# A second issue order for the first twelve head pairs of a fused attention and MLP kernel

## The chip, the cores and the metric

The kernel runs on one core of a Trainium2 chip. Its time is the device time of one execution in microseconds (us); the medians are over several executions. Five engines work beside each other, each through its own queue in order: TensorE (PE, matmuls), VectorE (DVE), ScalarE (ACT), GpSimd (POOL) and SyncE (SP, which here only issues DMAs). An instruction that waits holds up everything behind it in its own queue.

## What is computed

```python
q_n, k_n = rmsnorm(q, g_q), rmsnorm(k, g_k)          # over head_dim
attn = softmax(q_n @ k_n.T / sqrt(64)) @ v           # 8 batches x 12 heads x 448 tokens x 64
x = attn.transpose(0, 2, 1, 3).reshape(8 * 448, 768)
h = x @ w_in                                         # 768 -> 2048
out = (h * sigmoid(1.702 * h)) @ w_out               # 2048 -> 768, float32
```

## The kernel before

The unit of the attention is a pair of heads of one batch; pair i belongs to batch i // 6, so that the first twelve pairs are batches 0 and 1. A pair passes through these tasks, which the code names by letters (they are declared from line 730 on with `od.add`):

- **L** loads q, k and v of the pair (three DMAs of 224 KB, lines 515 and 518, issued by SP; k of pair 0 by ACT). **S** squares q and k (line 525 on ACT or 522 on POOL), **R** sums the squares (534, DVE), **Q** makes the inverse root: for pairs 0 to 5 by logarithm and exponential on ACT (545, 546), later for three pairs at once by a seed on DVE (**Q0**, 553 and 555) and eight small instructions on POOL (566 to 569).
- **N** multiplies by it (576, on DVE or POOL, once for q and once for k), **V** casts v (586 on DVE, 589 on POOL), **T** turns q and k (599, PE, for the first twelve pairs; later a DMA transpose, 611), **KQ** and **K** take them to SBUF (603, 606).
- **C** are the scores (643, PE), **E** the exponentials (653 and 651, ACT), **P** the product with v (664, PE), **O** the division (674, 675, DVE), **B** and **X** turn the result into columns of x (690, PE, and 694, DVE; later a DMA transpose, 697). The pairs of batch 0 are worked in two halves of the queries, (C,i,0,..) and (C,i,1,..), the other pairs whole.
- The MLP has **F** (first matmul, 875, 16 blocks of the 2048 columns per batch), **H** (tanh, 885, ACT), **G** (gate, 897, DVE), and for the second matmul **Y** (905) with the first three token tiles, and products P1 to P7 (965) over sums S1 to S5 (956, DVE) and differences TT of the weights (945, DVE) for the others. **WI** and **WO** load w_in and w_out in four parts each (842, 848; POOL issues them, and they land as bf16).

No engine's order is written out by hand. `_Order.run` (line 64) is a small list scheduler that runs while the program is built. Each task has an engine, a planned duration, a key and the tasks that it depends on; when an engine is free in the plan, the ready task with the lowest key is emitted next. What the chip gets is only the resulting order on each queue, with the waits that the data need. Nothing of the planned times is in the program. Three tables steer it: `KEYS` (line 223) gives a task's key, `AT` (line 325) the earliest planned time of a load, and the tasks in `ON` (line 335) go to the other of two engines (S to POOL instead of ACT; N and V to the other of DVE and POOL). Loads and stores are planned with queues of transfers, `share` (line 97) saying how fast each proceeds while others do.

`fill` (line 494) puts dummy matmuls on PE (128x256, line 500) where the plan has a gap ahead of a PE task: 24 and 10 at the very start, and after it

```python
n = idle * FILL / 213 if now < 14000.0 else idle * FILL_GAPS / 110
```

of them. They are real instructions in the queue. Three PSUM banks (`w`) serve T, B, F, Y and the products, one (`o`) serves P, so that a P must wait until DVE has divided the one before it; two pairs of banks (`sc`) serve the scores.

Of the kernel before, what the change touches and what calls it, by code (L numbers as in the profile page):

```python
# [26 lines left out]
class _Order:  # L27
# [36 lines left out]
    def run(self):  # L64
# [26 lines left out]
        queues = {"sw": [], "hw": [], "act": []}  # L91
        moved_to = 0.0
# [4 lines left out]
        def share():  # L97
            n = len(heads())
            return 1.3 / 2 if n == 2 and not queues["sw"] else 1.0 / n

        def next_moved():
            h = heads()
            when = [q[0].there for q in queues.values() if q and q[0].there > moved_to]
            when += [moved_to + t.rest / share() for t in h]
            return min(when) if when else None

        def move_to(now):
            nonlocal moved_to, seq
            while moved_to < now:
                n = next_moved()  # L110
                until = now if n is None else min(now, n)
                h = heads()
                for t in h:
                    t.rest -= (until - moved_to) * share()
# [109 lines left out]
    'g': 14.22, 'gT': -28.28, 'gG': 10.29, ('S', 0, 0): 33.65, ('R', 0, 0): -27.2, ('S', 0, 1):  # L224
    11.09, ('R', 0, 1): 12.24, ('Q', 0): 30.36, ('N', 0, 0): -6.12, ('N', 0, 1): -30.37, ('V',
    0): -7.89, ('T', 0, 0): -31.78, ('T', 0, 1): -29.53, ('KQ', 0): -10.97, ('K', 0): -11.43,
    ('S', 1, 0): 9.57, ('R', 1, 0): -27.21, ('S', 1, 1): 33.28, ('R', 1, 1): 9.51, ('Q', 1):
    33.27, ('N', 1, 0): 9.56, ('N', 1, 1): 11.7, ('V', 1): -5.89, ('T', 1, 0): 57.36, ('T', 1,
    1): 54.48, ('KQ', 1): -6.09, ('K', 1): -5.86, ('S', 2, 0): 32.41, ('R', 2, 0): -5.94, ('Q',
    2): 15.94, ('N', 2, 0): -4.94, ('N', 2, 1): -13.33, ('V', 2): 10.47, ('T', 2, 0): 55.3,  # L230
    ('T', 2, 1): 17.1, ('KQ', 2): -6.5, ('K', 2): -4.7, ('S', 3, 0): -3.51, ('R', 3, 0): -11.44,
    ('Q', 3): 33.8, ('N', 3, 0): -27.91, ('N', 3, 1): -14.89, ('V', 3): -5.47, ('T', 3, 0):
    19.15, ('T', 3, 1): 18.23, ('KQ', 3): 58.1, ('K', 3): -9.14, ('S', 4, 0): 33.8, ('R', 4, 0):
    57.84, ('Q', 4): 34.16, ('N', 4, 0): 23.2, ('N', 4, 1): 9.27, ('V', 4): -10.25, ('T', 4, 0):
    -3.92, ('T', 4, 1): 18.9, ('KQ', 4): -7.69, ('K', 4): 59.82, ('S', 5, 0): 18.65, ('R', 5,
    0): -7.68, ('Q', 5): 22.81, ('N', 5, 0): 1.27, ('N', 5, 1): 43.71, ('V', 5): -16.35, ('T',
    5, 0): -40, ('T', 5, 1): 16.66, ('KQ', 5): -8.39, ('K', 5): -9.71, ('L', 6, 0): 54.32, ('L',
    6, 1): 54.14, ('L', 6, 2): 54.15, ('S', 6, 0): -24.61, ('R', 6, 0): -9.13, ('N', 6, 0):
    -16.87, ('N', 6, 1): -1.42, ('V', 6): -24.19, ('T', 6, 0): -37.32, ('T', 6, 1): 56.1, ('KQ',
    6): -17.12, ('K', 6): -15.91, ('L', 7, 0): 55.06, ('L', 7, 1): 57.25, ('L', 7, 2): 55.05,  # L240
    ('S', 7, 0): -17.15, ('R', 7, 0): 31.45, ('N', 7, 0): 3.06, ('N', 7, 1): -23.94, ('V', 7):
    -24.2, ('T', 7, 0): 52.6, ('T', 7, 1): 22.24, ('KQ', 7): -20.86, ('K', 7): 9.99, ('L', 8,
    0): 54.79, ('L', 8, 1): 57.74, ('L', 8, 2): 53.4, ('S', 8, 0): 44.16, ('R', 8, 0): 31.27,
    ('Q0', 8): -1.5, ('Q', 8): -10, ('N', 8, 0): 3.5, ('N', 8, 1): 19.46, ('V', 8): -20.98,
    ('T', 8, 0): 27.35, ('T', 8, 1): 59.99, ('KQ', 8): -20.38, ('K', 8): -21.01, ('L', 9, 0):
    53.95, ('L', 9, 1): 55.46, ('L', 9, 2): 55.45, ('S', 9, 0): -9.31, ('R', 9, 0): -17.4, ('N',
    9, 0): -3.91, ('N', 9, 1): -10.14, ('V', 9): 22.05, ('T', 9, 0): -32.5, ('T', 9, 1): -35.1,
    ('KQ', 9): 21.57, ('K', 9): -38.08, ('L', 10, 0): 57.72, ('L', 10, 1): 59.75, ('L', 10, 2):
    60, ('S', 10, 0): -10.41, ('R', 10, 0): 19.25, ('N', 10, 0): 27.28, ('N', 10, 1): -1.35,
    ('V', 10): -15.43, ('T', 10, 0): -30.6, ('T', 10, 1): -36.19, ('KQ', 10): -4.09, ('K', 10):  # L250
    -37.28, ('L', 11, 0): 59.99, ('L', 11, 1): 59.99, ('L', 11, 2): 55.44, ('S', 11, 0): -13.26,
    ('R', 11, 0): 29.44, ('Q0', 11): 25.43, ('Q', 11): -9.79, ('N', 11, 0): 24.78, ('N', 11, 1):
    3.73, ('V', 11): 3.33, ('T', 11, 0): -37.35, ('T', 11, 1): -37.08, ('KQ', 11): -32.1, ('K',
    11): 24.13, ('C', 0, 0, 0): -31.61, ('E', 0, 0, 0): 59.86, ('C', 0, 0, 1): -26.54, ('E', 0,
    0, 1): 56.76, ('P', 0, 0, 0, 0): 53.97, ('P', 0, 0, 0, 1): -27.58, ('P', 0, 0, 0, 2):
    -30.53, ('P', 0, 0, 0, 3): -27.58, ('O', 0, 0, 0): -5.47, ('B', 0, 0): -40, ('X', 0, 0):
    -11.15, ('C', 1, 0, 0): -26.72, ('E', 1, 0, 0): -2.87, ('C', 1, 0, 1): 57.55, ('E', 1, 0,
    1): 16.48, ('P', 1, 0, 0, 0): 18.9, ('P', 1, 0, 0, 1): 18.63, ('P', 1, 0, 0, 2): 18.63,
    ('P', 1, 0, 0, 3): 18.89, ('O', 1, 0, 0): -13.5, ('B', 1, 0): 20.2, ('X', 1, 0): -11.33,
    ('C', 2, 0, 0): -40, ('E', 2, 0, 0): 18.66, ('C', 2, 0, 1): 20.21, ('E', 2, 0, 1): 13.02,  # L260
    ('P', 2, 0, 0, 0): 15.34, ('P', 2, 0, 0, 1): -36.54, ('P', 2, 0, 0, 2): -39.14, ('P', 2, 0,
    0, 3): -39.14, ('O', 2, 0, 0): -0.47, ('B', 2, 0): -39.81, ('X', 2, 0): -5.02, ('C', 3, 0,
    0): 17.29, ('E', 3, 0, 0): 39.33, ('C', 3, 0, 1): -39.63, ('E', 3, 0, 1): 38.35, ('P', 3, 0,
    0, 0): 15.85, ('P', 3, 0, 0, 1): 43.01, ('P', 3, 0, 0, 2): 17.41, ('P', 3, 0, 0, 3): 18.15,
    ('O', 3, 0, 0): -10.7, ('B', 3, 0): 15.63, ('X', 3, 0): 0.44, ('C', 4, 0, 0): -4.69, ('E',
    4, 0, 0): 38.96, ('C', 4, 0, 1): 38.48, ('E', 4, 0, 1): 24.48, ('P', 4, 0, 0, 0): -33.37,
    ('P', 4, 0, 0, 1): 60, ('P', 4, 0, 0, 2): -31.73, ('P', 4, 0, 0, 3): 17.26, ('O', 4, 0, 0):
    0.31, ('B', 4, 0): 57.93, ('X', 4, 0): 41.32, ('C', 5, 0, 0): -31.71, ('E', 5, 0, 0): 17.88,
    ('C', 5, 0, 1): 15.57, ('E', 5, 0, 1): 35.94, ('P', 5, 0, 0, 0): 33.77, ('P', 5, 0, 0, 1):
    33.77, ('P', 5, 0, 0, 2): 33.77, ('P', 5, 0, 0, 3): 33.76, ('O', 5, 0, 0): -0.04, ('B', 5,  # L270
    0): -23.85, ('X', 5, 0): 33.63, ('C', 0, 1, 0): 14.17, ('E', 0, 1, 0): 39.32, ('C', 0, 1,
    1): -39.73, ('E', 0, 1, 1): 33.79, ('P', 0, 1, 0, 0): -36.96, ('P', 0, 1, 0, 1): -33.38,
    ('P', 0, 1, 0, 2): 60, ('P', 0, 1, 0, 3): -14.87, ('O', 0, 1, 0): 60, ('B', 0, 1): 54.78,
    ('X', 0, 1): 34.24, ('C', 1, 1, 0): -36.97, ('E', 1, 1, 0): -39.74, ('C', 1, 1, 1): -36.95,
    ('E', 1, 1, 1): 24.11, ('P', 1, 1, 0, 0): 33.76, ('P', 1, 1, 0, 1): -23.7, ('P', 1, 1, 0,
    2): -22.7, ('P', 1, 1, 0, 3): -23.86, ('O', 1, 1, 0): -21.46, ('B', 1, 1): -39.64, ('X', 1,
    1): 0.33, ('C', 2, 1, 0): -27.46, ('E', 2, 1, 0): -31.49, ('C', 2, 1, 1): -18.62, ('E', 2,
    1, 1): 37.85, ('P', 2, 1, 0, 0): -39.65, ('P', 2, 1, 0, 1): -40, ('P', 2, 1, 0, 2): 21.69,
    ('P', 2, 1, 0, 3): -40, ('O', 2, 1, 0): -14.64, ('B', 2, 1): -36.82, ('X', 2, 1): -4.18,
    ('C', 3, 1, 0): 55.19, ('E', 3, 1, 0): 37.86, ('C', 3, 1, 1): 60, ('E', 3, 1, 1): 23.18,  # L280
    ('P', 3, 1, 0, 0): -18.63, ('P', 3, 1, 0, 1): -13.68, ('P', 3, 1, 0, 2): -13.69, ('P', 3, 1,
    0, 3): -11.57, ('O', 3, 1, 0): 39.32, ('B', 3, 1): 22.25, ('X', 3, 1): -18.47, ('C', 4, 1,
    0): -15.41, ('E', 4, 1, 0): 9.01, ('C', 4, 1, 1): -25.6, ('E', 4, 1, 1): -9.3, ('P', 4, 1,
    0, 0): -36.38, ('P', 4, 1, 0, 1): -36.83, ('P', 4, 1, 0, 2): -36.39, ('P', 4, 1, 0, 3):
    -34.65, ('O', 4, 1, 0): -20.37, ('B', 4, 1): 20.64, ('X', 4, 1): 22.61, ('C', 5, 1, 0):
    -16.67, ('E', 5, 1, 0): 42.7, ('C', 5, 1, 1): 51.97, ('E', 5, 1, 1): 36.5, ('P', 5, 1, 0,
    0): 47.97, ('P', 5, 1, 0, 1): 48.4, ('P', 5, 1, 0, 2): 60, ('P', 5, 1, 0, 3): 55.7, ('O', 5,
    1, 0): 25.18, ('B', 5, 1): -40, ('X', 5, 1): 21.57, ('C', 6, None, 0): 24.44, ('E', 6, None,
    0): -11.29, ('E', 6, None, 1): -16.82, ('C', 6, None, 2): 24.41, ('E', 6, None, 2): -7.71,
    ('E', 6, None, 3): -16.82, ('P', 6, None, 0, 0): -40, ('P', 6, None, 0, 1): -40, ('P', 6,  # L290
    None, 0, 2): -40, ('P', 6, None, 0, 3): -39.93, ('O', 6, None, 0): 23.74, ('P', 6, None, 1,
# [933 lines left out]
```

## Time and profile before

| what | us |
|---|---|
| median of four runs (lowest to highest) | 428.72 (428.24 to 429.49) |
| the profiled execution | 428.15 |
| its span from first to last instruction | 426.4 |
| PE busy in the span | 408.8 |
| ACT, DVE, POOL busy | 302.7, 297.1, 189.8 |
| dummy matmuls: 89, of which 55 stand behind the first 34 | |
| first F of batch 1 (marks the end of the stage that the change orders) | 92.83 |

The profile is one execution. A busy share is an average over stages; a "wait" in it is the idle time of an engine ahead of an instruction, with the instruction that ended it. The median of the runs lies 0.57 us over the profiled execution, and the span 1.75 us under it.

### The profile page before, as it was taken

How to read it: one execution, taken by the hardware profiler on the slowest of the kernel's cores; microseconds unless marked ns; L12 is line 12 of the kernel's file. 1: busy time of each engine (PE TensorE's matmuls, PEld its weight loads, DVE VectorE, ACT ScalarE, POOL GpSimd, SP SyncE). 2: the span in 40 equal slices, each digit the busy share in tenths (PEclk: the TensorE clock that was granted, in tenths of full speed). 3: DMA queues.
4: the chain of work that ended last, by engine and by line, in shares of the span. 5: the costliest groups of instructions: out<-in, count | busy, mean ns of one | idle time of the engine just before them, and what ended most of it. 6: DMA issues, size and time to landing. Idle time of an engine off the chain costs nothing.

```text
span 426.4 us, 10048 instructions
## 1 busy us (share of the span) xinstructions
PE 408.8 (96%) x3874; PEld 241.6 (57%) x3874; DVE 297.1 (70%) x584; ACT 302.7 (71%) x437; POOL 189.8 (45%) x277
## 2 busy tenths in 40 slices
PE   6899899999989999999999999999999999999995
PEld 4558686655555555555555555555555555565553
DVE  5967988579988667965787577764676555655663
ACT  4898788869978699978986589967775477604400
POOL 5396843657387473853636345553642100000000
PEclk9999999999999999999999999999999999999999
DMA  8999999375659989666646687566433630121023
GB/s 238 270 259 245 264 251 246 94 163 128 136 118 216 196 208 213 154 166 156 171 102 160 167 220 164 136 139 165 75 77 95 158 90 13 23 67 38 0 75 92
DMA packets 101555, 63.38 MB, mean 149 GB/s; under 512 B 54916, under 2 KB 101508, under 8 KB 101508
## 3 DMA queue, kind: packets, MB, share of 16 engines
q1 hardware_dynamic: 93712, 55.88, 54.0%
q0 software_dynamic: 7296, 6.29, 9.1%
q8 instruction: 30, 0.49, 0.5%
q10 hardware_dynamic: 500, 0.57, 0.4%
q14 instruction: 17, 0.14, 0.1%
HBM read 45.61 MB, written 11.01 MB: 133 GB/s over the span
## 4 chain that ended last, share of the span: by engine, by line
PE 78%; DVE 10%; ACT 5%; issue 3%; DMA 3%; SPq 0%; POOL 0%; DVEq 0%; ACTq 0%
PE w L875 30%; PE w L965 17%; PE o L664 10%; PE sc L643 9%; PE sc L965 4%; PE w L905 4%; DVE late L956 3%; PE sc L875 2%; ACT att L653 2%; DMA raw<-in_k_dram 2%; ACT sq L525 2%; DVE obs L675 1%; DVE ssq L534 1%; DVE g L897 1%; DVE w_out_s L945 1%
## 5 line engine op out<-in xcount | busy, mean ns | idle before, releaser
L651 ACT ACTIVATE att<-sc 112x896 bf16<-112x896 f32 x168 | 145.8, 916 | 33.9 <-PE sc L643 33.4
L875 PE MATMUL w<-xt,w_in_s 128*128 128x448 bf16 (+1 forms) x810 | 150.7, 330 | 0.1
L875 PEld LDWEIGHTS <-w_in_s 128*128 128x128 bf16 x864 | 78.1, 97 | 54.2 <-issue 6.7
L664 PEld LDWEIGHTS <-att 112*128 112x128 bf16 x1536 | 72.5, 98 | 49.3 <-issue 18.2
L576 POOL TENSOR_TENSOR row<-raw,rs 112x512 bf16<-112x512 f32 x80 | 89.5, 1139 | 23.1 <-DMA qk<-row 13.7
L897 DVE SCALAR_TENSOR_TENSOR g<-th,w 128x448 bf16<-128x448 f32 x119 | 72.5, 616 | 27.1 <-ACT th L885 26.5
L885 ACT ACTIVATE th<-w 128x448 f32<-128x448 f32 x119 | 64.7, 548 | 26.6 <-PE w L875 25.1
L589 POOL TENSOR_TENSOR vx<-vraw,ones 112x512 bf16<-112x512 f32 x35 | 36.5, 1042 | 97.9 <-PE o L664 62.0
L664 PE MATMUL o<-vx,att 112*128 112x65 bf16 x1280 | 74.0, 194 | 4.9 <-DVE obs L675 4.8
L534 DVE TENSOR_REDUCE ssq<-sq 112x16 f32<-112x1024 f32 (+1 forms) x50 | 58.4, 1170 | 10.0 <-ACT sq L525 8.8
L525 ACT ACTIVATE sq<-raw 112x1024 f32<-112x1024 f32 (+1 forms) x43 | 44.5, 1035 | 9.7 <-DMA raw<-in_k_dram 5.8
L643 PE MATMUL sc<-qk 64*128 64x448 bf16 (+1 forms) x360 | 46.9, 342 | 1.6 <-DVE qk L606 1.4
L675 DVE TENSOR_TENSOR obs<-o,rcp 112x256 bf16<-112x256 f32 x96 | 40.7, 424 | 3.3
L965 PEld LDWEIGHTS <-g 128*128 128x128 bf16 x336 | 29.9, 97 | 19.6 <-issue 3.0
L674 DVE RECIPROCAL rcp<-o 112x4 f32<-112x4 f32 x96 | 17.0, 177 | 33.2 <-PE o L664 32.6
L965 PEld LDWEIGHTS <-late 128*128 128x128 bf16 x328 | 28.8, 97 | 18.3 <-issue 2.6
L965 PE MATMUL w<-w_out_s,g 128*128 128x384 bf16 x176 | 33.5, 325 | 0.0
L965 PE MATMUL w<-w_out_s,late 128*128 128x384 bf16 x152 | 29.7, 326 | 0.2 <-DVE late L956 0.2
L965 PE MATMUL w<-late 128*128 128x384 bf16 x144 | 28.1, 326 | 0.0
L978 DVE TENSOR_SCALAR osb<-w 128x384 f32<-128x384 f32 x25 | 13.9, 556 | 16.9 <-PE w L965 16.8
L566 POOL TENSOR_TENSOR t<-rs 112x48 f32<-112x48 f32 x28 | 8.2, 292 | 37.3 <-DVE rs L555 36.2
L617 ACT ACTIVATE qk<-qk,gG 128x448 bf16<-128x448 bf16 x36 | 24.2, 676 | 0.7 <-DMA qk<-row 0.7
(92 smaller groups left out, 379.3 us busy)
## 6 DMA issues: line engine op xcount, KB each, us to landing
raw<-in_q_dram SPq DMA_DIRECT2D x44, 224.0 KB, 3.8
raw<-in_k_dram SPq DMA_DIRECT2D x43, 224.0 KB, 4.5
vraw<-in_v_dram SPq DMA_DIRECT2D x42, 224.0 KB, 3.7
w_in_s<-in_moe_w_in_dram POOLq DMA_DIRECT2D x4, 768.0 KB, 15.6
w_out_s<-in_moe_w_out_dram POOLq DMA_DIRECT2D x4, 768.0 KB, 20.5
out_dram<-osb SPq DMA_DIRECT2D x14, 168.0 KB, 2.4
out_dram<-osb SPq DMA_DIRECT2D x12, 144.0 KB, 2.4
out_dram<-osb SPq DMA_DIRECT2D x12, 120.0 KB, 2.5
```

The source lines that it names most:

```text
L525: nc.scalar.activation(out=sq[i % N_SQ][:SS, part], in_=raw[turn(i, N_RAW, K_RAW)][:SS, part], func=ACT.Square)
L534: nc.vector.reduce_sum(out=ssq_of[g0][:SS, i - g0, part], in_=sq[i % N_SQ][:SS, part], axis=AX.X)
L576: eng.tensor_tensor(out=row_ring[i % N_QKN][:SS, gi].rearrange("p n (h d) -> p h n d", h=2), in0=raw[turn(i, N_RAW, K_RAW)][:SS, gi], in1= ...
L589: nc.gpsimd.tensor_tensor(out=vx[:, :, :D], in0=vr, in1=ones[:SS, :].to_broadcast([SS, 2 * NS, D]), op=ALU.mult)
L643: nc.tensor.matmul(sc[:, hp, j * SH:j * SH + n], lhsT=qkw[r, k0:k0 + WIN], rhs=qk[r, 0, qs], start=True, stop=True)
L651: nc.scalar.activation(out=att[:SS, t, :, :S], in_=sc, func=ACT.Exp)
L664: nc.tensor.matmul(os_[u, w][:, x, :], lhsT=att_of(u)[:SS, kc, hp, qs * SS:qs * SS + WIN], rhs=vx_ring[turn(i, N_V, K_V)][:SS, hp, kc, :], ...
L675: nc.vector.tensor_tensor(out=to[:SS, :, w, :] if h is None else to[:SS, :2].rearrange("p n h d -> p (n h) d"), in0=o[:SS, :, :D], in1=rcp ...
L875: nc.tensor.matmul(gps[b, m][:, j * SH:j * SH + n], lhsT=w_in_s[:, ki, f * 128:(f + 1) * 128], rhs=xT[b][:, ki, lo:lo + n], start=(ki == 0 ...
L885: nc.scalar.activation(out=th[:, :], in_=gps[b, m][:, :S], func=ACT.Tanh, scale=0.851)
L897: nc.vector.scalar_tensor_tensor(out=g_of[b // 2][:, f:f + len(g), lo:lo + n], in0=view(ths.pop((b, m))[:, :]), scalar=1.0, in1=view(gps.p ...
L965: nc.tensor.matmul(held[to], lhsT=lhs[:, ko, :], rhs=y[:, ko, :], start=first and ko == 0, stop=ko == NK - 1, skip_group_check=not first)
```

## The change

It alters the planner's model of two queues and the three tables, and through them the order of instructions. No operation, size or buffer is changed, and the program has the same instructions apart from dummy matmuls.

```diff
-        def share():
+        def share(t):
             n = len(heads())
-            return 1.3 / 2 if n == 2 and not queues["sw"] else 1.0 / n
+            if n != 2:
+                return 1.0 / n
+            return 0.65 if not queues["sw"] else 0.69 if t.eng == "POOL" else 0.47
...
-                    t.rest -= (until - moved_to) * share()
+                    t.rest -= (until - moved_to) * share(t)
...
 KEYS = {
-    'g': 14.22, 'gT': -28.28, 'gG': 10.29, ('S', 0, 0): 33.65, ('R', 0, 0): -27.2, ('S', 0, 1):
+    'g': 31.44, 'gT': 10.91, 'gG': 46.18, ('S', 0, 0): -6.54, ('R', 0, 0): 34.8, ('S', 0, 1):
...
+    36.66, ('WO', 0): 39.14, ('WO', 1): 5.06, ('WO', 2): 9.91, ('WO', 3): 13.51, ('L', 13, 2):
+    -21.98, ('F', 0, 10): 6.06, ('F', 0, 14): 20.03, ('F', 0, 15): -39.94, ('G', 0, 3): 33.87,
...
-ON = {('S', 0, 1), ('N', 0, 1), ('S', 1, 0), ('N', 1, 1), ('N', 2, 0), ('N', 2, 1), ('V', 2), ('N', 3, 1), ('N', 4, 0), ('V', 5), ('S', 6, 0), ('N', 6, 0), ('S', 8, 0), ('V', 9), ('V', 10), ('N', 11, 0), ('N', 11, 1)}
+ON = {
+    ('N', 0, 1), ('N', 1, 0), ('N', 10, 0), ('N', 10, 1), ('N', 2, 0), ('N', 2, 1), ('N', 5, 1),
+    ('S', 0, 1), ('S', 4, 0), ('S', 6, 0), ('S', 7, 0), ('S', 8, 0), ('S', 9, 0), ('V', 1),
+    ('V', 10), ('V', 11), ('V', 2), ('V', 4), ('V', 7)}
```

All keys of the first twelve pairs and all earliest times of `AT` have other values, and the F, H and G of batch 0 and the loads of pairs 12 to 15 have keys of their own for the first time. What this does to the queues is read from the built programs:

- **Engines.** The squares of pairs 4, 7 and 9 go from ACT to POOL, the first half of pair 1's from POOL to ACT. Of the N of the first twelve pairs, seven are on DVE (nine before); of the V six, as before, but others.
- **Start.** Pair 1 is turned, scored and exponentiated before pair 0. DVE has `KQ1, R2, KQ0, K1, K0` where it had `KQ0, K0, R2, V1, KQ1, K1`.
- **POOL** after the first N: `WI0 WI1 V1 S4 N3 N3 V2 N4 N4 V4 N5 WI2 WI3 S6 WO0 S8 S7 Q8 N6 V8 N6 N8 N7 V6 N8 N7 S9 WO1 WO2 WO3` (before: `WI0 WI1 V2 N3 N4 V5 N5 N5 WI2 WI3 S6 WO0 V6 S8 V7 Q8 N7 N6 V8 N7 N8 N8 V11 WO1 WO2 WO3`).
- **DVE** around the seed of pairs 6 to 8: `R8 G(0,0) R7 Q0` (before: `R7 ... R8 Q0 G(0,0)`).
- **PE** ahead of the first scores of pair 6: eight F of batch 0 (before: six). Dummy matmuls: 78 (before 89), the first 34 unchanged.
- **Later.** From the Y of batch 0 on, the attention runs about one pair further ahead of the MLP: `P1` of token tile 3, the first product after F(1,15), stands behind both values of pair 15 (before: behind half of pair 14). From the MLP of batch 3 on (pair 25 in the attention) the orders are the same on every engine. The loads' order is the same for the first 18 issues of SP and differs after that.

## The prediction

> **What bounds the kernel now.** I read the page first, then the busy times by stage, then the time line of each engine up to 93 us, task by task.
>
> ```profile
> span 426.4 us, 10048 instructions
> PE 408.8 (96%) x3874; PEld 241.6 (57%) x3874; DVE 297.1 (70%) x584; ACT 302.7 (71%) x437; POOL 189.8 (45%) x277
> ```
>
> PE is the bound: 17.6 us of the span are idle. Its real work is fixed by the diff, so the time can change only through PE's idle gaps and its dummy matmuls. By stage (columns: PE, PEld, DVE, ACT, POOL busy, clock, DMA share, GB/s):
>
> ```profile
> 9.40:24.70 15.30, 13.08 (x185) 8.99 (x186) 14.89 (x31) 13.29 (x22) 8.77 (x8) 1.00 1.15 267
> 24.70:36.60 11.90, 11.35 (x162) 7.52 (x163) 6.91 (x18) 11.75 (x14) 9.61 (x9) 1.00 1.17 257
> 36.60:47.70 11.10, 9.71 (x142) 8.67 (x140) 9.39 (x21) 6.81 (x11) 8.40 (x14) 1.00 1.19 247
> 47.70:70.50 22.80, 22.36 (x313) 18.45 (x311) 20.08 (x45) 20.94 (x29) 12.98 (x19) 1.00 1.21 253
> 92.80:120.00 27.20, 27.13 (x232) 14.33 (x230) 23.12 (x39) 25.62 (x41) 16.84 (x27) 1.00 0.51 124
> 120.00:142.00 22.00, 19.77 (x201) 11.44 (x200) 19.32 (x34) 16.45 (x21) 17.60 (x21) 1.00 0.81 188
> ```
>
> From 9.4 to 70.5 us PE idles 4.6 us (sum of the differences), and 55 dummies run, at 0.11 us each in a row: 5.9 us. These 10.5 us are all that the ordered stage can give; from 47.7 on PE is nearly full. In 24.7 to 36.6 ACT is full (11.75 of 11.90), so there a dummy costs nothing and only ACT work counts. The tasks behind it:
>
> ```profile
> 24.68 7.66 ACT L653 ACTIVATE att<-sc 112x896 bf16<-112x896 f32 x9
> 32.24 1.05 ACT L525 ACTIVATE sq<-raw 112x1024 f32<-112x1024 f32 x1
> 33.19 3.36 ACT L653 ACTIVATE att<-sc 112x896 bf16<-112x896 f32 x4
> 36.62 0.55 ACT L885 ACTIVATE th<-w 128x448 f32<-128x448 f32 x1
> 47.65 1.72 ACT L651 ACTIVATE att<-sc 112x896 bf16<-112x896 f32 x2 [1.52 <-PE sc L643]
> ```
>
> The square between two rows of exponentials is pair 7's; it holds up (H,0,0), the first tanh, by its length. The last line is the first exponential of pair 6. It was late because its norms were:
>
> ```profile
> 32.13 1.88 POOL L522 TENSOR_TENSOR sq<-raw 112x1024 f32<-112x1024 f32 x1
> 38.64 0.27 POOL L566 TENSOR_TENSOR t<-rs 112x48 f32<-112x48 f32 x1 [3.09 <-DVE rs L555]
> 41.63 1.04 POOL L576 TENSOR_TENSOR row<-raw,rs 112x512 bf16<-112x512 f32 x1
> 42.63 1.49 POOL L576 TENSOR_TENSOR row<-late,rs 112x512 bf16<-112x512 f32 x1
> 46.25 0.26 PE L690 MATMUL w<-ident,obs 112*128 112x112 bf16 x2 [1.39 <-DVE qk L606]
> ```
>
> POOL waits 3.09 us for the seed on DVE, then needs 41.6 - 38.6 for Q8 and about 1 us for each norm. PE's largest gap, 1.39 us, stands there: DVE, behind R9, divided (P,2,1) late.
>
> **The change step by step, to the first F of batch 1 (92.83 us before).** Durations are those of the rows, back-to-back: E 0.81, S on ACT 0.95, on POOL 1.93 (pair 6) or 1.88, R 1.21, N 0.68 on DVE and 1.04 on POOL, F 1.15, C 0.2 to 0.5, P of a half pair 0.6.
>
> 1. *Start.* Both parts of pair 1's square on ACT and its R without V0 between them bring Q1 from 8.74 to 8.15. But K1 now stands behind R2 and KQ0, so the first scores wait to 12.3 (10.84 before), and in ACT's queue the first E stands behind Q2 and S3: R2 ends at 11.5, Q2 12.1, S3 13.1, so the first E starts at 13.0 (11.25 before). Loss here: 1.75 us. From there ACT runs E1, E1, E0, Q3, E0, E2 to 17.55, waits about 0.5 for (C,2,0,0) behind (P,0,0), and without S4 goes on Q4, S5, E3, E3, Q5, table to about 24.3 (24.67 before): S4 gave back 0.95, tighter waits the rest. Gain 0.4, between -0.5 (S4 on POOL late) and 0.9.
> 2. *ACT's full stretch.* Twelve E at 0.81 are ready in time by this reckoning (N5 on DVE at 24.9, T5 25.7, (C,0,1,1) 26.1). S7 is off ACT: 0.95. (H,0,0) ends at 35.0 instead of 37.16. Moves counted so far: 1.2 to 2.2 us.
> 3. *PE around 36 to 47.* (F,0,0) at 33.1, four more F to 39.4, F5 40.8 to 42.0, F6 43.6, F7 to 47.0; the first scores of pair 6 at 47.0 as before (47.05), but with eight F behind them and not six: 2 x 1.15 = 2.3 us. The gap of 1.39 is gone since on DVE that division no longer stands behind R9.
> 4. *POOL.* S6, S8, S7 end at 33.1; (G,0,0) at 35.6, R7 36.8, seed 37.2, Q8 to 40.1 (41.55 before). Eight instructions follow to the last norm of pair 7, 48.2; PE reaches its turn at 48.4. So 2.3 us hold, and the 0.41 us that PE waited for (T,8,1) goes: at (C,7,0) PE is ahead by 52.69 - 52.0 = 0.7 and by two F, 3.0 us in all.
> 5. *To F(1,0).* PE's remaining work is known, and it had no gap here (22.36 of 22.80, then 22.30 of 22.30). ACT has S9 off its queue, WO1 leaves POOL at 50.1 as before (50.06), so the second part of w_out lands about 61.8 as before and is wanted at about 66.5. T10 meets its norms on DVE within 0.5 us. I take 2.6 of the 3.0 us.
>
> The dummies (11 fewer, 1.2 us) are inside these sums. DMA: the loads come at 0.77 us each until 16.4, at 1.95 while w_in is loaded; the first 18 are the same, and S4, S7, S8, S9 and S10 have theirs 1 to 6 us early at that pace. At run time `AT` holds nothing back.
>
> [...]
>
> **After the stage.** The stretch 120 to 142 has 2.2 us of PE idle, most of it in two waits:
>
> ```profile
> PE o L664 <- DVE obs L675: 4.8, 7, 1.2
> ```
>
> A P waited for a division that stood behind three sums on DVE. The new order puts (O,16,0) behind S1, S2, S3 again, but with one more half pair of P, and so later on PE: reckoned 0 to 0.75 instead of 1.25. The second (0.98) has only S2 ahead of its division. Against that, ACT has to do four more E in the stretch of F of batch 1. Value taken: +0.5, between -1 and +1.5. The stalls from pair 28 on repeat, since the order there is the same; for the change of order in batch 2 I take -0.3.
>
> Sum: 2.6 + 0.5 - 0.3 = 2.8 us. The profiled execution would be 428.15 - 2.8 = 425.35, and with the 0.57 us between it and the median, 425.9.
>
> **The rivals.** All against 428.72.
>
> *Slower: POOL becomes the bound between 37 and 51 us.* It now has three more long squares and eight instead of six instructions between Q8 and the last norm, and the seed waits for (G,0,0), so for (H,0,0). [...] The trace shows it: N beside N takes 1.49 on POOL and 1.02 on DVE, against 1.04 and 0.68 alone. If ACT's start is not made good, (H,0,0) ends at 37.2 as before, R7 at 39.0, Q8 42.4; six N at 1.49 and two V at 1.04 bring the last norm to 53.4, and PE, due at 48.4, waits 5.0. Of 3.0 us, -2.0 are left; with step "after", +0.5: 430.2. It decides from a last norm at 51.5 on. [...] Chance 0.12.
>
> *No change: given back later.* ACT is 25.62 of 27.20 busy in 92.8 to 120, and the new order asks four more E (3.2 us) there. If PE waits there or for w_out, the lead of 2.6 is lost: 428.6. Against it: PE gets the same four scores and values between its F. Chance 0.18.
>
> *All of it.* Every gap of 9.4 to 70.5 (4.6) and the dummies saved (1.2), less the 0.5 that the start shows: 423.4. Chance 0.10.
>
> *Forecast* 425.9, 0.60, own range 424.3 to 427.6 (steps 1 and 5 and the stretch after, each at its bounds).
>
> A planner that misses the chip is inside these: the order is only as good as its durations. One such place: w_in's last part lands at 43.2, and F6 is wanted at 43.6; each us later costs one.
>
> **Numbers.** About 0.2% (0.86 us) is what a measurement of this kernel can tell from no change. Faster by more: forecast nearly whole 0.58, "all" 0.10, a part of "given back" 0.04: 0.72. Same 0.16. Slower 0.12. The range leaves out most of the slower case and part of "all": 423.5 to 429.0.
>
> **What would show it.** Right: (H,0,0) ending near 35 and the first E near 13.0; eight F ahead of pair 6's scores at about 47; no PE gap over 0.5 us from 40 to 70; F(1,0) near 90.2. Wrong: the last norm of pair 7 after 49; a PE wait on w_in ahead of F6; F(1,0) near 90 but a longer wait of P on the division after it.

## The result, and the profile after

| | median us | single runs | ratio to before, 95% interval |
|---|---|---|---|
| before | 428.64 | 428.01 to 430.88 | |
| changed | 427.69 | 424.44 to 431.91 | 0.9963 (0.9950 to 0.9975) |

The change makes the kernel faster. By the ratio it is some 1.6 us (0.37% of 428.6); the medians lie only 0.95 us apart. The new median is inside the range on record and 1.8 us above the forecast. Single runs now lie 7.5 us apart instead of 2.9; the ratios, here and below, leave out runs more than 1.5% above the fastest of their kernel (two of these 44, three of the twelve of x2 below). The profiled execution took 426.98 us (1.17 less than that of before). Its page:

```profile
span 425.2 us, 10013 instructions
...
PE 408.2 (96%) x3863; PEld 240.3 (57%) x3863; DVE 293.4 (69%) x583; ACT 299.1 (70%) x434; POOL 192.1 (45%) x281
```

The busy times by stage, in the stretches shown for before:

```profile
9.40:24.70 15.30, 12.49 (x182) 8.67 (x182) 13.74 (x28) 11.96 (x20) 12.28 (x12) 1.00 1.16 248
24.70:36.60 11.90, 11.16 (x162) 7.56 (x157) 8.43 (x22) 11.58 (x15) 8.04 (x7) 1.00 1.17 255
36.60:47.70 11.10, 9.30 (x127) 8.46 (x126) 8.09 (x18) 6.47 (x11) 8.66 (x15) 1.00 1.19 247
47.70:70.50 22.80, 22.09 (x306) 17.74 (x303) 19.66 (x45) 19.41 (x28) 16.38 (x22) 1.00 1.19 257
...
120.00:142.00 22.00, 21.85 (x219) 12.57 (x216) 19.32 (x36) 17.62 (x23) 14.54 (x21) 1.00 0.92 205
```

From 9.4 to 70.5 us PE idles 6.06 us, more than the 4.60 of before, though it runs eleven dummies fewer; from 120 to 142 it idles 0.15 instead of 2.23. So the ordered stage, for which the order was made, gave nothing here, and the gain comes from a stretch that follows it. Marks on PE say the same, once the work ahead of them is counted. F(1,0) starts 0.49 us later (93.32; 92.83 before), but behind four more score matmuls, half of pair 12's, which are 0.5 us of PE: the stage comes out even. F(2,0), the second half of the first F of batch 2, starts 1.23 us earlier (144.83; 146.06 before) and behind 16 value and four score matmuls more, some 1.1 us: a lead of about 2.3. About 1.1 of it is then given back. PE's waits behind this mark, after (the first five lines, one of them ACT's) and before:

```profile
160.18 1.06 ACT L544 ACTIVATE sq<-raw 112x1024 f32<-112x1024 f32 x1 [1.29 <-DMA raw<-in_k_dram]
163.33 0.36 PE L662 MATMUL sc<-qk 64*128 64x448 bf16 x2 [0.22 <-ACT att L670]
164.01 0.43 PE L683 MATMUL o<-vx,att 112*128 112x65 bf16 x8 [0.32 <-DVE obs L694]
181.06 0.43 PE L683 MATMUL o<-vx,att 112*128 112x65 bf16 x8 [1.01 <-DVE obs L694]
318.53 0.43 PE L683 MATMUL o<-vx,att 112*128 112x65 bf16 x8 [0.68 <-DVE obs L694]
...
181.93 0.43 PE L664 MATMUL o<-vx,att 112*128 112x65 bf16 x8 [0.82 <-DVE obs L675]
319.65 0.43 PE L664 MATMUL o<-vx,att 112*128 112x65 bf16 x8 [0.35 <-DVE obs L675]
```

The old order has no wait of PE at 163 to 164. In the new one ACT waits 1.29 us for the load of a square shortly ahead of it (160.18), which is the pattern that the ordered stage shows too, below. PE's other waits of this part differ by less than 0.02 us. What is left of the lead is the 1.2 us of the spans.

What held the ordered stage up is seen on four engines. PE's time line:

```profile
43.62 1.31 PE L894 MATMUL w<-xt,w_in_s 128*128 128x224 bf16 x12 [1.65 <-DVE xt L713]
...
46.19 1.31 PE L894 MATMUL w<-xt,w_in_s 128*128 128x224 bf16 x12
...
49.31 0.55 PE L662 MATMUL sc<-qk 64*128 64x448 bf16 x4
...
51.98 0.36 PE L618 MATMUL w<-ident,row 112*128 112x112 bf16 x4 [0.71 <-POOL sq L541]
```

The lines are F5, F6, the first scores of pair 6 and T(7,1). T(7,1) is put down to S9 on POOL, of which it reads nothing; KQ7 on DVE ended at the same 51.93, and x0, x1 and x7, with 0.7 to 0.8 us of wait there, name KQ7. F5, with the longest gap, needs a PSUM bank that X(1,1) on DVE, a copy of xt, has to empty. DVE and, ahead of it, ACT:

```profile
42.16 1.22 DVE L553 TENSOR_REDUCE ssq<-sq 112x16 f32<-112x1024 f32 x1 [2.14 <-ACT sq L544]
43.30 0.26 DVE L713 COPY xt<-w 128x224 bf16<-128x224 bf16 x1
43.48 1.14 DVE L916 SCALAR_TENSOR_TENSOR g<-th,w 128x448 bf16<-128x448 f32 x2
```

```profile
41.07 1.06 ACT L544 ACTIVATE sq<-raw 112x1024 f32<-112x1024 f32 x1 [2.19 <-DMA raw<-in_q_dram]
42.04 0.96 ACT L904 ACTIVATE th<-w 128x448 f32<-128x448 f32 x2
```

The chain reads backwards: F5 at 43.62 waits for X(1,1) (43.30), which stands on DVE behind R10 (42.16), which waits 2.14 us for S10 (41.07) on ACT, which waits 2.19 us for its load. The tanh (H,0,3) waits behind S10 as well. R6 on DVE, POOL's long squares and the first instruction of Q8:

```profile
31.26 1.21 DVE L553 TENSOR_REDUCE ssq<-sq 112x16 f32<-112x1024 f32 x1
...
27.74 1.89 POOL L541 TENSOR_TENSOR sq<-late 112x1024 f32<-112x1024 f32 x1 [0.88 <-DVE late L625]
32.56 1.88 POOL L541 TENSOR_TENSOR sq<-raw 112x1024 f32<-112x1024 f32 x1 [2.04 <-DVE rcp L693]
35.38 1.89 POOL L541 TENSOR_TENSOR sq<-raw 112x1024 f32<-112x1024 f32 x1 [0.94 <-DMA raw<-in_k_dram]
39.05 0.27 POOL L585 TENSOR_TENSOR t<-rs 112x48 f32<-112x48 f32 x1 [1.78 <-DVE rs L574]
```

The squares are S6, S8 and S7. S7 ends at 37.27, where 33.1 was reckoned: it waits 0.94 for its load, and S8 ahead of it began at 32.56 and not at once after S6, since it writes the buffer of squares that R6 on DVE had to read until 32.47 (there are two; the row names the instruction of DVE behind R6).

### The profile page after: what moved, and what is told of

It reads as the page before. It is cut to its first block, busy times and chain, and to the rows that moved or that the text cites. A ratio compares the mean times of both kernels' runs of the same rounds, so it can differ in the third digit from the quotient of the medians.

```text
span 425.2 us, 10013 instructions
## 1 busy us (share of the span) xinstructions
PE 408.2 (96%) x3863; PEld 240.3 (57%) x3863; DVE 293.4 (69%) x583; ACT 299.1 (70%) x434; POOL 192.1 (45%) x281
## 4 chain that ended last, share of the span: by engine, by line
PE 73%; DMA 9%; DVE 9%; POOL 4%; issue 2%; ACT 1%; SPq 0%; DVEq 0%; POOLq 0%; ACTq 0%
PE w L894 26%; PE w L984 19%; PE o L683 10%; PE sc L662 8%; DMA raw<-in_k_dram 5%; PE sc L984 4%; PE w L924 3%; DVE late L975 3%; PE sc L894 2%; DMA raw<-in_q_dram 2%; POOL row L595 2%; DVE ssq L553 2%; DMA late<-in_v_dram 2%; DVE obs L694 1%; POOL sq L541 1%
## 5 line engine op out<-in xcount | busy, mean ns | idle before, releaser
L595 POOL TENSOR_TENSOR row<-raw,rs 112x512 bf16<-112x512 f32 x82 | 88.6, 1105 | 17.9 <-DMA qk<-row 14.8
L608 POOL TENSOR_TENSOR vx<-vraw,ones 112x512 bf16<-112x512 f32 x35 | 37.4, 1067 | 89.6 <-PE o L683 57.8
L544 ACT ACTIVATE sq<-raw 112x1024 f32<-112x1024 f32 (+1 forms) x41 | 42.3, 1038 | 14.5 <-DMA raw<-in_k_dram 9.2
```

Source lines behind the costliest of these rows:

```text
L544: nc.scalar.activation(out=sq[i % N_SQ][:SS, part], in_=raw[turn(i, N_RAW, K_RAW)][:SS, part], func=ACT.Square)
L595: eng.tensor_tensor(out=row_ring[i % N_QKN][:SS, gi].rearrange("p n (h d) -> p h n d", h=2), in0=raw[turn(i, N_RAW, K_RAW)][:SS, gi], in1= ...
L608: nc.gpsimd.tensor_tensor(out=vx[:, :, :D], in0=vr, in1=ones[:SS, :].to_broadcast([SS, 2 * NS, D]), op=ALU.mult)
```

## The experiments

All times are compared with runs of the kernel before on the same chip. The theory: *the new order puts squares on the edge of the arrival of their loads*; what is sure in its gain is the stretch 120 to 142. The rivals: POOL's squares are the loss; the TensorE clock is; the gain is given back later.

| run | median us | ratio, 95% interval | F(1,0) in its profile |
|---|---|---|---|
| x0 changed, again | 427.58 | 0.9972 (0.9947 to 0.9997) | 93.80 |
| x1 changed, S10 and R10 later | 425.83 | 0.9947 (0.9921 to 0.9973) | 91.48 |
| x2 x1, loads reordered too | 429.88 | 0.9985 (0.9952 to 1.0019) | 96.16 |
| x3 before, two sums later | 426.27 | 0.9937 (0.9919 to 0.9955) | 93.33 |
| x4 changed, short v | 424.71 | 0.9926 (0.9899 to 0.9954) | 92.67 |
| x5 before, short v | 428.34 | 0.9998 (0.9986 to 1.0010) | 92.98 |
| x6 before, DVE's order mended | 425.15 | 0.9926 (0.9906 to 0.9945) | 95.56 |
| x7 changed, DVE's order mended | 422.28 | 0.9852 (0.9830 to 0.9875) | 91.02 |
| x8 before, S7 on POOL | 428.41 | 1.0005 (0.9996 to 1.0013) | 93.82 |
| x9 changed, more dummies | 426.71 | 0.9955 (0.9938 to 0.9972) | 95.76 |
| x10 x2, N(5,1) on POOL | 425.53 | 0.9942 (0.9920 to 0.9964) | 92.46 |
| x11 x7, N(5,1) on POOL, dummies | 422.56 | 0.9868 (0.9855 to 0.9881) | 92.52 |

In all but x0 the order of the tasks is written out and fixed, so that nothing moves but what the diff shows. F(1,0) can be compared between orders of one kind; the new order has the 0.5 us of scores more ahead of it.

### x0: the changed kernel again

> The changed kernel once more, as the baseline of this set. Theory (loads on the edge): in the profiled run of the changed kernel PE waited 1.65 us ahead of (F,0,5), because the first tanh group's PSUM bank came late behind S10 on ACT, which waited 2.19 us for its load; and S7 and S8 on POOL waited 2.98 us for theirs. If this profile shows loads landing every 0.77 us at the start, as before the change, those waits should be shorter than 1 us in all and F(1,0) should start near 91; if they land every 0.9 us, the waits come back and F(1,0) starts near 93.3. Rival (POOL is the loss): the gap ahead of (F,0,5) and F(1,0) near 93.3 come whatever the loads do. Ratio to the kernel before: 0.9965, between 0.994 and 0.998.

The loads came every 0.94 us (mean of the 3rd to the 15th of SP), as they had every 0.91 in the first profile; the waits came back, 2.48 on ACT and 1.73 on PE, and F(1,0) at 93.80. The case of fast loads didn't come up, so this run does not yet choose. (Of the 2.98 us in the text, 2.04 were S8's wait for R6 and not for a load.)

### x1: S10 and R10 later

```diff
 ACT order
-H(0,2) S(10) H(0,3) H(0,4) E(5,1,1) E(5,1,0) H(0,5) E(3,1,1) H(0,6)
+H(0,2) H(0,3) H(0,4) E(5,1,1) E(5,1,0) H(0,5) E(3,1,1) S(10) H(0,6)
 DVE order: R(10) from behind G(0,2) to behind O(3,1,0)
```

> The changed kernel's own order with two places changed: S10 later on ACT, behind (E,3,1,1), and R10 later on DVE, behind (O,3,1,0). Theory (loads on the edge): S10 no longer waits for its load in front of (H,0,3), so PE's gap of 1.65 us ahead of (F,0,5) falls below 0.5 and the time falls by about 1 to 1.5 us against the changed kernel, ratio to the kernel before about 0.993. Rival (POOL's squares are the loss): pair 7's last norm stays at 50.1, PE waits for it instead of for the bank, and the time stays within 0.3 us of the changed kernel. Rival (given back later): the gap goes, but F(1,0) comes near 92 and the time doesn't change by more than 0.3 us.

This text puts the cause on ACT, behind S10; by the rows above the path to F5 goes on over R10 and X(1,1) on DVE. The run moves both, so it doesn't tell the two apart. The gap ahead of F5 is gone; the stretch 36.6 to 47.7 of this run reads

```profile
36.60:47.70 11.10, 11.05 (x154) 9.80 (x152) 8.82 (x22) 7.27 (x12) 8.57 (x16) 1.00 1.20 248
```

PE is busy 11.05 of 11.10, against 9.30, F(1,0) starts 1.8 to 2.3 us earlier and the median falls by 1.75 (427.58 to 425.83; the intervals overlap). POOL's squares are untouched, so at least this part of the loss isn't theirs.

### x2 and x10: loads of q and k earlier, and where it went wrong

```diff
 SP order
-L(7,v) L(6,q) L(8,q) L(8,k) L(7,q) L(7,k) L(10,v) L(10,k) L(10,q) L(8,v)
+L(6,q) L(8,q) L(8,k) L(7,q) L(7,k) L(10,k) L(10,q) L(7,v) L(10,v) L(8,v)
 DVE order: V(7) to behind V(10)
 x10 also: N(5,1) from DVE to POOL, behind N(5,0)
```

> As the run with S10 later, and also the loads of q and k of pairs 7 and 10 one or two places earlier in SP's queue (the v loads of these pairs go behind them, and V7 on DVE behind V10). Theory (loads on the edge): S7 on POOL has its load one place earlier, so it ends at 36.0 or earlier instead of 37.27, the seed, Q8 and the last norm of pair 7 come about 1 us earlier (49 instead of 50.1), and the time is another 0.3 to 1 us below that of the run with S10 later alone: ratio about 0.991. Rival (POOL's length, not its loads): S7 ends less than 0.4 us earlier, and the time is that of S10 later alone.

A miss: 4 us slower than x1. Its trace, all engines from 25.7 us:

```profile
26.40 3.37 DVE L595 TENSOR_TENSOR row<-late,rs 112x512 bf16<-112x512 f32 x1
...
27.09 0.28 PE L519 MATMUL w<-zeros,ident 128*128 128x256 bf16 x1
27.28 1.93 POOL L541 TENSOR_TENSOR sq<-late 112x1024 f32<-112x1024 f32 x1
...
29.82 0.27 PE L618 MATMUL w<-ident,row 112*128 112x112 bf16 x2 [2.45 <-DVE row L595]
```

N(5,1) on DVE takes 3.37 us instead of 0.68, until 0.56 us after the end of S6 on POOL; PE waits 2.45 for it. S6's load was in earlier here, so S6 followed at once on the issue of w_in (26.45 to 27.28). That alone is not the condition: in x4 and x7 S6 followed at once too, and N(5,1) took 0.68 (more on this at the rivals).

> The run with reordered loads again, with N(5,1) on POOL, behind N(5,0), instead of on DVE. In that run N(5,1) took 3.37 us on DVE while POOL issued w_in and then squared pair 6 at once, and PE waited 2.45 us for it. Theory (DVE's norm was blocked by POOL): with both norms on POOL each takes 1.04, PE's gap at 27 is below 0.5 us, most runs lie near the 424.2 to 424.6 that its fastest runs had, median 424.5, ratio 0.991. Rival (the reordered loads hold up something else): the median stays near 429.9.

With N(5,1) on POOL the long norm and the gap at 27 us are gone, and the median is 4.35 us lower. It doesn't reach the expected 424.5. In its profile w_in's last part, issued a norm later on POOL, lands at 45.0 (44.0 in x1), and F6 waits for it:

```profile
45.05 1.32 PE L894 MATMUL w<-xt,w_in_s 128*128 128x224 bf16 x12 [1.01 <-DMA w_in_s<-in_moe_w_in_dram]
```

For F6 the prediction had said that each microsecond of w_in later costs one.

### x3: the kernel before without its two waits at 124 and 137 us

```diff
 DVE order
-S3(0,3) U(0,3,0) O(15,0) S4(0,3)
+U(0,3,0) O(15,0) S3(0,3) S4(0,3)
-S3(0,5) U(0,3,1) O(17,0)
+U(0,3,1) O(17,0) S3(0,5)
```

> The kernel before with its own order and two places changed on DVE: two of the third sums of squares of batch 1 go behind the divisions (O,15) and (O,17). Theory (the certain part of the gain lies in 120 to 142 us): PE's waits of 1.25 and 0.98 us for a division go, the rest stays, so the time falls by 1.5 to 2.2 us, ratio 0.9955 (0.995 to 0.9965), which is as much as the whole change gave. Rival (PE then waits for something else in this stretch, or the sum comes late in its turn and holds up the norm of batch 1's end): the idle of PE in 120 to 142 stays above 1.5 us and the ratio above 0.998.

```profile
120.00:142.00 22.00, 22.00 (x236) 13.22 (x235) 19.11 (x36) 17.50 (x22) 19.10 (x22) 1.00 0.79 201
```

No idle time is left in the stretch, and the median falls by 2.16 us: two instructions moved on DVE give more than the whole change (0.9937 against 0.9972 on the same chip, where the intervals overlap, and 0.9963 over all its runs). As the changed kernel has lost these waits too, the rest of its new order is by the medians 1.3 us worse than the old one (427.58 - 426.27), not 2.6 better. A part of this lies behind the ordered stage: the waits from 163 us on that the first profile has more than before are 1.1 us, in x0's profile 0.2.

### x4 and x5: loads that land earlier, in both orders

```diff
-nc.sync.dma_start(out=vraw[...][:SS], in_=src)
+h, n = (1, 1) if 6 < i < 12 else (2, NS)
+nc.sync.dma_start(out=vraw[...][:SS, :h, :n], in_=src[:, :h, :n])
```

> The changed kernel with its own order, but the loads of v of pairs 7 to 11 move an eighth of their bytes (the rest of these v tiles is left as it was, so the outputs of those pairs are not the reference's). The loads of q and k behind them land earlier: those of pair 7 by about 1.5 us, of pair 10 by about 3. Theory (loads on the edge): ACT's wait of 2.2 to 2.5 us ahead of S10 and PE's gap of 1.65 us ahead of (F,0,5) go, POOL waits less than 0.5 us ahead of S7, F(1,0) starts at 91 or before, and the ratio to the kernel before is 0.991 to 0.993. Rival (POOL's squares are the loss): F(1,0) stays at 93 or later and the ratio at 0.996 or above. A second way to lose, seen with the reordered loads: N(5,1) on DVE took 3.37 us instead of 0.68 when S6 followed the issue of w_in on POOL at once; if S6's earlier load brings this about here too, a gap of 2.4 us stands at 27 and the ratio is 0.998 or above in most runs.

> The kernel before with the same shortened loads of v of pairs 7 to 11. Theory (loads on the edge in the new order alone): the order of before has slack, so it gains little: ratio 0.998 to 1.0. If it gained 2 us as well (0.995), the loads would hold up both orders alike, and the theory would say nothing of the change.

This pair tests the loads; what it leaves out, the rest of v, makes the results of those pairs wrong, so only its times count. The order of before gains nothing (0.9998), the new one goes to 0.9926 (x0: 0.9972; the intervals overlap a little), and eight of its twelve runs lie between 423.5 and 425.1. S10 no longer waits; ACT in x4:

```profile
39.35 0.54 ACT L905 ACTIVATE th<-w 128x448 f32<-128x448 f32 x1 [0.61 <-DVE ssq L573]
39.79 1.05 ACT L545 ACTIVATE sq<-raw 112x1024 f32<-112x1024 f32 x1
```

PE had no gap ahead of F5. F(1,0) misses the expected 91, at 92.67: this execution had lost 2.4 us at 7.9, where ACT waited 1.62 for a load of pair 1 and the norms came late, and its first E began 1 us later (14.67) than in the changed kernel. S7 no longer waits for its load, but ends at 37.31 all the same, because S8 ahead of it waits 2.94 for R6.

### x6 and x7: both orders mended on DVE

```diff
 DVE order, both: S3(1,0), S3(1,3), S3(2,0), S3(2,3) behind
 O(23,0), O(28,0), O(35,0), O(40,0), that stood behind them
 x6 also: x3's two moves, and R(9) from ahead of KQ(6) to behind K(6)
 x7 also: x1's two moves
```

> The kernel before in its own order, with DVE alone changed: the two third sums of batch 1 behind the divisions as in the earlier run, the same for four more sums (ahead of pairs 23, 28, 35 and 40), and R9 behind K6, so that the division of (2,1) doesn't stand behind it. Taken from its trace: 1.25 + 0.98 + 0.82 + 0.33 + 0.91 + 0.36 of waits, and 1.39 of the gap at 45 us. Expected: 424 us, ratio 0.990 (0.988 to 0.993), with a spread as small as that of the kernel before. If the waits only move, no lower than the 426.3 of the two sums alone.

> The changed kernel with S10 and R10 later and the same four later sums behind their divisions. Taken from the trace: the waits of 1.01, 0.31, 0.90 and 0.37 us on top of what S10 later gave. Expected: 423.5 us, ratio 0.988 (0.985 to 0.993); the spread of single runs stays some 4 us wide, since its start is that of the changed kernel.

x7 is better than expected and the fastest of the study. Its page and its largest waits:

```profile
span 419.2 us, 10013 instructions
...
PE 407.4 (97%) x3863; PEld 240.3 (57%) x3863; DVE 292.6 (70%) x583; ACT 299.5 (71%) x434; POOL 193.4 (46%) x281
```

```profile
PE w L618 <- DVE row L595: 1.8, 2, 1.0
PE w L519 <- POOL ident masks.py:199: 1.4, 1, 1.4
```

x6 fell short (424 expected, 425.15): R9 was not what held up the division of (2,1). PE in x6:

```profile
45.72 0.26 PE L690 MATMUL w<-ident,obs 112*128 112x112 bf16 x2 [1.39 <-DVE qk L606]
45.82 0.68 PE L664 MATMUL o<-late,att 112*128 112x65 bf16 x16
47.38 0.34 PE L690 MATMUL w<-ident,obs 112*128 112x112 bf16 x2 [0.88 <-DVE g L897]
```

The 1.39 is there as before, for DVE stood 1.67 us in KQ6 ahead of that division, waiting for pair 6's transposes; R9, moved on, made a new gap of 0.88. From 47.01, in the second gap, the clock was at a half for 6.8 us (0.97 over the stretch 36.6 to 47.7 and 0.87 over 47.7 to 70.5), and F(1,0) came at 95.56 in this execution.

### x8: pair 7's square on POOL, alone

```diff
-ON = {('S', 0, 1), ...
+ON = {('S', 7, 0), ('S', 0, 1), ...
```

> The kernel before in its own order, with one part of the change alone: pair 7's square on POOL (between V6 and S8) instead of ACT. The step of the prediction (S7 off a full ACT is 0.95): (H,0,0) ends 0.95 earlier than in the kernel before, (F,0,0) starts at about 34.3, and as the seed of pair 8 waits behind (G,0,0), the first scores of pair 6 come earlier too, so 0.7 to 0.95 us reach F(1,0): ratio 0.998. Rival (POOL pays): S7 and S8 on POOL wait for loads or run into the seed, the first scores of pair 6 stay where they are, the F ahead of them wait, and the ratio is 0.999 to 1.001. In the changed kernel S7 on POOL waited 0.94 us for its load at 34.4, but there its load stood later in the queue.

Nothing (1.0005). The 0.95 us on ACT turned into a wait on DVE:

```profile
34.80 1.22 DVE L534 TENSOR_REDUCE ssq<-sq 112x16 f32<-112x1024 f32 x1 [0.46 <-POOL sq L522]
35.94 0.27 DVE L694 COPY xt<-w 128x224 bf16<-128x224 bf16 x1
36.12 0.17 DVE L674 RECIPROCAL rcp<-o 112x4 f32<-112x4 f32 x1
36.33 0.42 DVE L675 TENSOR_TENSOR obs<-o,rcp 112x256 bf16<-112x256 f32 x1
36.67 0.27 DVE L694 COPY xt<-w 128x224 bf16<-128x224 bf16 x1
```

R7 waits for the longer square, the copies of xt for batch 0 stand behind it, and F0 needs them: PE waits 0.58 us there, at 36.26. (The profile is of the slowest of the eleven runs, whose first E came 0.76 us late; from the table's end to the end of (H,0,0) it needs 12.7 us, against 12.5 before.)

### x9 and x11: the clock at the start

```diff
 dummies ahead of T(1,0): 10 -> 17, ahead of T(0,0): 1 -> 8
 x11: x7 with these dummies, and N(5,1) on POOL
```

> The changed kernel in its own order, with seven more dummy matmuls in each of PE's two gaps at 8.3 and 9.9 us. Rival (the TensorE clock makes the spread and the loss): three of four profiles of this order without the shortened loads showed a stretch of 3.41 us at half the clock from about 11 us on, right behind these gaps; with the gaps filled it is gone, the mean clock is 0.998 or more in most runs, the median falls by 1.5 us or more and the spread shrinks to about 2 us. Theory (loads on the edge): at 11 to 14 us PE isn't the bound, so the half clock there costs 0.5 us at most (F(1,0) was 0.48 later with it than without): the clock may rise, but the median stays within 0.6 us of the changed kernel (427.6) and the spread stays at 5 us or more.

Seven of eight runs now have a mean clock of 0.997 or more (x0: four of twelve; its profile, with half the clock from 10.7 to 14.2 us, has 0.995), so by this number the early half-clock stretch went. The median is 0.9 us below that of x0, with overlapping intervals, between the two theories; seven runs lie within 2.7 us, one at 430.26. So the clock has a part, which these runs can't size. It is not what held up the first profile of the changed kernel: there it was full from 7.0 us on, until 423.4, shortly before the end (1.00 in all its rows above). The profile fell on another cost: with S6's load in early, N(5,1) took 3.37 us again, in the changed kernel's own order, and the clock fell to a half in PE's gap of 2.45 (four transposes ahead of it took 0.37 us, four behind it 0.55):

```profile
24.70:36.60 11.90, 8.81 (x101) 5.20 (x103) 7.32 (x13) 7.78 (x10) 4.72 (x5) 0.71 1.17 255
```

> The changed kernel with S10 and R10 later and the four later sums behind their divisions, as in the fastest run so far (422.3), with N(5,1) on POOL as well and the fourteen dummies at the start. Theory: two sources of spread less, so a median of 421.5 to 422.5 with single runs within 2.5 us, ratio 0.984. Rival: POOL, one norm fuller at 25 us, starts S6 1 us later and loses it again: 423.

As fast as x7 within the intervals, with single runs within 1.0 us (four runs). F(1,0) is later than in x7, as F6 waits 1.22 us for w_in like in x10.

## Why the prediction was half right

**Direction and range held, the account did not.** 2.6 us were to come from the ordered stage and 0.2 from the rest. At equal work of PE the first profile shows none from the stage, 2.3 from the stretch behind it, and 1.1 of these given back. That the number fell inside the range is luck: a gain that was valued at 0.5 stood in for the one on which the forecast rested.

**Step 1 (start), wrong by 1.1.** The first E came at 13.69, not 13.0, and the load of ACT's table behind the last Q ended at 25.37, not 24.3. In x7, where loads landed every 0.84 us, they were 13.08 and 24.77. By this pair of profiles 0.6 us go with the loads' pace, and 0.1 to 0.5 were missing in my sum.

**Step 2 (ACT's full stretch), right in this order, not as an effect of S7 alone.** From the table's end to the end of (H,0,0) the new order takes 10.8 us (reckoned 10.7; before 12.5). x8 shows that the same move in the old order is worth nothing, since R7 and the copies behind it wait instead. I had costed the squares on ACT and on POOL (1.05 and 1.93 us a square in the rows of before, 2.6 us more for three, against 0.95 each off a full ACT and POOL's waits of 3.09 and 3.60), not what stands behind S7's reader on DVE; the same pair, an R and the copy of xt behind it, made the gap ahead of F5.

**Step 3 (PE 36 to 47), the failed step.** F5 was put at 40.8 and came at 43.62. The claim under it, that S4, S7, S8, S9 and S10 have their loads "1 to 6 us early at that pace", was wrong. It took a pace from the one execution shown, and that was the quickest of all: 0.77 us a load, where the other thirteen profiles, of old and new orders, have 0.83 to 0.99. S10's load landed at 40.97 and S7's at 35.25; the loads at the same places of SP's queue had landed at 36.09 and 30.90 in that one execution. S4 waited for its load as well, 1.68 us. The old order doesn't care (x5; x3 with 0.98 us a load had F(1,0) only 0.5 later). The eight F ahead of pair 6's scores were there as forecast, at 49.3 instead of 47.0. Of the 1.39 gap the end was forecast rightly and its cause wrongly (x6: KQ6, not R9). With S10 behind E(3,1,1), x7 shows the step as reckoned: F5 at 41.04, F6 at 43.63 and the scores at 46.74.

**Step 4 (POOL), late by 1.9 to 4.2.** S7 was to end at 33.1; it ended at 37.27 (35.71 in x7, with its load in time). Left out was S8's wait for R6 to free the buffer, 2.0 to 2.9 us. Pair 7's last norm came at 50.09 (49.08 in x7), past the 49 that was to show this step wrong; but PE did not wait for it, in either profile.

**Step 5 (F(1,0)).** 90.2 forecast, 93.32 measured: 1.2 of it were there at F0, 1.65 came ahead of F5, 0.71 ahead of T(7,1), and 0.4 were made good. x7's 91.02 comes near: with the 0.5 us of scores it is 2.3 ahead of the old order there, where 2.6 were forecast. So, in an execution with quick loads and with S10 out of the way, the forecast of the stage nearly holds.

**After the stage: mis-sized.** Value taken +0.5, and -0.3 for batch 2; the first profile has about 2.3, and -1.1 from there to the end. x3 prices the two waits at 2.2 us, and in the changed kernel both are gone: S2 and S3 ahead of (O,16,0) take 0.69 and 0.68 us, where those ahead of (O,15,0) in the old order took 1.42 and 1.53 beside norms on POOL, and a half pair more of P covers them; (O,18,0) stands ahead of its S3.

**The rivals.** POOL as the bound: in the profile of before a norm on POOL took 1.49 beside one on DVE and 1.04 alone, and with none queued on DVE there I had reckoned with 1.04; the six norms took 1.04 each, so it did not come about. "Given back later": the number is near (428.6), and 1.1 us were given back, but from another lead, that of 120 to 142 us; ahead of 120 there was none to lose. At another place came a cost that I had not reckoned: 3.37 us for N(5,1) on DVE, against the 1.49 that I took as the worst. In the seven profiles with N(5,1) on DVE, it was long in the two (x2 and x9) where S6's wait for its load was over 0.22 and 0.47 us before N(5,1) began, and 0.68 in the five where it was over by at most 0.09 before, or later. In both long cases N(5,1) ended 0.56 us after S6 on POOL (29.77 and 29.21 in x2, 29.12 and 28.56 in x9). With the norm on POOL (x10) the long one is gone; what held it on DVE is not in the trace.

**The spread.** The new order meets late loads at S10 (x0) and early ones at N(5,1) (x9), and pays 1.7 to 2.5 us and some clock for either. With both mended and the dummies (x11), the spread of four runs was 1.0. Which share of the 7.5 us each has is open, because only the profiled executions have a trace. But every run's mean clock is on record, and a stretch of 3.4 us at half, as x0 and x1 had, lowers it by 0.004 (0.5 x 3.4 of 426 us): of the 44 runs the ten with 0.997 or more have a median of 425.6, the seven under 0.99 one of 430.3. By this estimate the long runs are those with about three such stretches; how much of their time is the clock's, and how much that of the gaps ahead of it, they don't tell.

## What to carry to other kernels

Compare a mark in two orders only with the work ahead of it counted. Where a change moves work nearer to its data, take the arrival of the data from several executions, and give each consumer at the head of an in-order queue a margin; what stands behind it (here a copy that frees a PSUM bank, for which PE waited 1.65 us) pays for a late load. When an operation changes its engine, follow its reader and what is queued behind that, not the two engines alone. Before a search over an order is trusted, two moves by hand out of the list of waits are worth a try: here two gave more than the change, and six on top of it another 4.8 us (0.9963 - 0.9852 of 428.6).

## What the runs showed of the hardware

The granted clock stood at a half for about 3.4 us, or twice that, in several profiles. Over 1.5 us each from 10.5 us on it was 0.58, 0.50 and 0.78 in x0, 0.71, 0.50 and 0.65 in x1, and 0.56, 0.50 and 0.81 in x2, which makes 3.42, 3.42 and 3.39 us at a half, from 10.7, 11.1 and 10.7 us on. x2 has it once more behind its gap of 2.45 (0.88, 0.50, 0.50, 0.98 from 30 us on: 3.42 us), x8 has 0.89 over 9.4 to 24.7 (3.4 us), x9 0.71 over 24.7 to 36.6 (6.9 us) with a gap of 2.45 in it, and x6 the 6.8 us from the second of its gaps (1.39 and 0.88) on.

PE was not idle throughout ahead of such a fall: from 7.5 to 10.5 us it was busy for 1.35 of the 3.0 us in x0, 0.95 in x1 and 1.39 in x2, and from 27 to 30 us in x2 for 0.55. Nor did the clock fall each time that PE had as little to do: the changed kernel's first profile has 1.27 us from 7.5 to 10.5, that of before 1.42 from 6.0 to 9.0, both at 1.00 there and up to 45 us. What decides between the two is not shown by these runs.
